# Attention's result transposed by VectorE in 32x32 blocks, and w_in's rows loaded in an order that matches

## The chip, the cores and the metric

The kernel runs on one core of a Trainium2 chip. A core has a matrix engine (TensorE, PE in the profile, with PEld for its weight loads), VectorE (DVE), ScalarE (ACT), GpSimd (POOL) and SyncE (SP), and 16 DMA engines that all queues share. SP and POOL issue nearly all transfers here. The metric is the device time of one execution in microseconds; lower is better. Every time below is in microseconds unless marked ns.

## The reference

Block-sparse attention over 4 batches, 8 heads, 768 positions and 64 channels a head, in blocks of 32 positions, followed by a feed-forward network of 512 to 2048 to 512 channels with an exact GELU:

```python
scores = scale * np.matmul(q, k.transpose(0, 1, 3, 2))
mask = np.abs(blk_i - blk_j) <= window                 # window = 1
mask = mask | (blk_i == 0) | (blk_j == 0) | (blk_i == n_blocks - 1) | (blk_j == n_blocks - 1)
for qb in range(n_blocks):
    for kb in sampled_blocks[qb]:                      # three drawn blocks for each
        mask[qb * block:(qb + 1) * block, kb * block:(kb + 1) * block] = True
attn = softmax(np.where(mask, scores, -1e9))
x = np.matmul(attn, v).transpose(0, 2, 1, 3).reshape(B * S, H * D)
h = x @ w_in
return (0.5 * h * (1.0 + erf(h / sqrt(2)))) @ w_out
```

So the first and the last block see everything (dense), and each of the other 22 sees its neighbours, the first, the last and three sampled blocks (sparse). Inputs are float32; the kernel computes in bfloat16 and accumulates in float32.

## The kernel before, in words

**Units.** The work is cut into eight units: one batch by one half of the positions (384 tokens). For each unit there is attention, which leaves `xT` (channels by tokens), then the first FFN product with GELU (`ffn1_step`, eight steps of two output tiles, 64 matmuls), then the second FFN product. The order of instructions on each engine is the order of the program; there is no scheduler. The second product of a unit is cut into 24 pieces of two matmuls (`ffn2_pieces`), which the next unit's attention draws one by one (`pieces`) to keep PE at work while it waits for others. The first unit has no such work, and draws idle matmuls instead (`idle_pieces`, L503).

**Groups and rounds.** A unit's attention has eight groups: two for the dense block, then five of two sparse blocks and one of a single one. A group passes through stages: scores on PE (`sc`, L339), a maximum on DVE (`nm`, L353 and L374), exponentials on ACT (`pp`, L385 and L388), transposes of the probabilities on PE (`tp`, L400) and their copy out of PSUM on ACT (`ps`, L407), the product with the values on PE (`av`, L431), and a division on DVE (`den`, `rec`, `xh`, L440 to L444). `attention` runs rounds `it`: in each, scores of group it+2, exponentials of it+1, transposes of group it, and the product of group it−`lag`. `lag` is 1, and 3 in the first unit, where values come late.

**From attention to `xT`.** `xh` has 32 queries times four pairs of heads on the partitions, and blocks and channels in columns. `stage_x` (L457 to L464) turns it one round later: one or two PE transposes of 128x128 into PSUM (`tx`, L459, from the pool `psT` that `tp` uses too), and a DVE copy into `xT` (L462). There is one more round for it at the end of a unit, with two pieces in front of it. The channels in `xT` then stand in their natural order, and so do `w_in`'s rows.

**Weights.** `load_w_in` loads columns 0 to 511, 512 to 1023 and 1024 to 2047 of `w_in` in three POOL DMAs, each for all four 128-row groups `ki`. The first is issued at the very start, the second after POOL's key copies (L632), the third after all value gathers of the first unit (L642).

**Values.** The values of a batch are written to a scratch in DRAM (L285) and read back: windows of neighbouring blocks (L310) and 33 gathers a unit of sampled blocks at places read from registers (L293). For the first unit SP and POOL share them; the second unit's (`second_values`) are all SP's. A memset by DVE in `second_values` (L651) writes the first window's place, so that SP's first window of the second unit waits for DVE to get there. POOL and SP each use eight completion semaphores in turn: a transfer waits for the one eight issues earlier on its queue.

## Time and profile before

| what | value |
|---|---|
| runs shown | 308.93 median of 3 (308.15 to 309.18) |
| profiled execution | 309.21, of which the span is 307.3 |
| PE busy | 284.0 (92%) |
| ACT busy | 207.8 (68%) |
| DVE busy | 197.1 (64%) |
| POOL busy | 126.7 (41%) |
| `tx` transposes on PE (L459) | 96, 14.8, 222 ns each |
| `xT` copies on DVE (L462) | 56, 14.9, 266 ns each |
| first FFN product on PE (L471) | 512, 88.6, 330 ns each |
| second FFN product on PE (L485) | 286 recorded, 81.9, 381 ns each |

The table shows busy time: for each engine the sum of the stretches in which it had work. A matmul's length includes the pipeline, so lengths of neighbours overlap, and what one matmul costs is better read from one start to the next. Lines of a timeline give the start, the length, the engine, the line and the tile written and read; in brackets stands how long the engine was idle before it and whose end it waited for. The granted clock of PE is a share of full speed. The first 60 microseconds hold the loads of the first batch, the first unit's attention and its first FFN product; from about 82 on one unit follows the other, some 33 apart.

### The profile page before, as it was taken

What the parts mean: (1) busy time and instruction counts of PE and PEld (TensorE: products, weight loads), DVE (VectorE), ACT (ScalarE), POOL (GpSimd) and SP (SyncE); (2) the same over time, 40 slices, a digit from 0 to 9 for tenths busy, and PEclk for the clock granted to TensorE, in tenths of its full rate; (3) what the DMA queues carried; (4) which work ended last, traced back from release to release, by engine and by line L of the source; (5) the groups of instructions that cost most, each with busy time, mean ns of one, the idle gap of its engine ahead of it and who ended that gap; (6) DMA issues with size and microseconds to landing.
All of it is one profiled execution on the core that took longest, in us unless ns stands there. A gap on an engine that the chain in (4) does not pass through costs nothing.

```text
span 307.3 us, 11604 instructions
## 1 busy us (share of the span) xinstructions
PE 284.0 (92%) x4476; PEld 173.0 (56%) x4526; DVE 197.1 (64%) x550; ACT 207.8 (68%) x443; POOL 126.7 (41%) x250
## 2 busy tenths in 40 slices
PE   6895969998999999999999989998999999999995
PEld 5443535555565566656565547555655656455784
DVE  6699454587594788878745868387818873684010
ACT  1485424588667896689668975788568965897620
POOL 8355926231556843824998172089603000000000
PEclk9999697999999999999999999999999999999999
DMA  7998899999278799799799958995632330000012
GB/s 94 197 217 149 182 209 228 228 225 194 87 234 176 166 215 222 267 253 200 186 242 168 229 111 282 260 241 145 174 81 63 64 101 3 35 4 36 34 36 68
DMA packets 55064, 48.45 MB, mean 158 GB/s; under 512 B 20385, under 2 KB 49058, under 8 KB 55010
## 3 DMA queue, kind: packets, MB, share of 16 engines
q1 hardware_dynamic: 35170, 30.86, 38.6%
q0 software_dynamic: 19408, 16.47, 33.6%
q8 instruction: 35, 0.57, 0.8%
q10 hardware_dynamic: 432, 0.39, 0.4%
q14 instruction: 19, 0.16, 0.2%
HBM read 45.63 MB, written 12.82 MB: 190 GB/s over the span
## 4 chain that ended last, share of the span: by engine, by line
PE 67%; ACT 12%; DMA 7%; issue 7%; SPq 2%; POOL 1%; DVE 1%; POOLq 0%; DVEq 0%
PE hp L471 28%; PE op L485 19%; ACT pp L385 8%; PE tp L400 5%; PE av L431 5%; PE sc L339 4%; PE op L519 3%; DMA w_in_sb<-in_moe_w_in_dram 3%; ACT ps L407 3%; DMA qn<-in_q_dram 3%; PE pt L245 2%; SPq L293 2%; PE tx L459 2%; DMA vscr<-vn 1%; ACT os L490 1%
## 5 line engine op out<-in xcount | busy, mean ns | idle before, releaser
L471 PE MATMUL hp<-xT,w_in_sb 128*128 128x384 bf16 x512 | 88.6, 330 | 2.4 <-DMA w_in_sb<-in_moe_w_in_dram 2.1
L485 PE MATMUL op<-w_out_sb,g 128*128 128x512 bf16 x286 | 81.9, 381 | 5.1 <-issue 4.6
L471 PEld LDWEIGHTS <-w_in_sb 128*128 128x128 bf16 x512 | 58.1, 115 | 30.7 <-DMA w_in_sb<-in_moe_w_in_dram 2.8
L475 ACT ACTIVATE g<-hp 128x768 bf16<-128x768 f32 x56 | 45.4, 811 | 38.5 <-PE hp L471 38.5
L385 ACT ACTIVATE pp<-sc,nm 128x256 bf16<-128x256 f32 x176 | 70.2, 492 | 0.0
L374 DVE TENSOR_REDUCE nm<-sc 128x4 f32<-128x1024 f32 (+1 forms) x48 | 54.5, 1135 | 12.1 <-ACT ps L407 10.3
L293 POOL DMA_DIRECT2D vg<-vscr x76 | 38.7, 513 | 35.9 <-PE sc L339 14.0
L407 ACT COPY ps<-tp 128x256 int32<-128x256 int32 (+2 forms) x114 | 36.1, 355 | 20.2 <-PE tp L400 18.4
L279 POOL COPY kg<-kT 128x128 bf16 x120 | 33.3, 332 | 30.3 <-PE sc L339 12.6
L400 PEld LDWEIGHTS <-pp 128*128 128x128 bf16 x448 | 31.2, 105 | 22.0 <-ACT pp L385 5.2
L400 PE MATMUL tp<-identity,pp 128*128 128x128 bf16 x448 | 40.3, 222 | 2.0
L485 PEld LDWEIGHTS <-g 128*128 128x128 bf16 x336 | 24.7, 97 | 21.9 <-issue 6.7
L353 DVE TENSOR_REDUCE nm<-sc 128x1 f32<-128x768 f32 x16 | 14.7, 952 | 31.8 <-PE sc L339 31.8
L431 PEld LDWEIGHTS <-ps 128*32 128x32 bf16 x1792 | 19.1, 97 | 18.9 <-issue 8.5
L431 PE MATMUL av<-vg,ps 128*32 128x65 bf16 x1408 | 21.4, 197 | 3.6 <-DMA vg<-vscr 2.4
L444 DVE TENSOR_TENSOR xh<-av,rec 128x256 bf16<-128x256 f32 (+1 forms) x56 | 21.6, 386 | 1.9
L462 DVE COPY xT<-tx 128x256 bf16<-128x256 bf16 (+1 forms) x56 | 14.9, 266 | 11.5 <-PE tx L459 11.4
L339 PE MATMUL sc<-kg,qT 64*32 64x256 bf16 (+1 forms) x704 | 18.7, 270 | 0.5 <-issue 0.5
L490 ACT COPY os<-op 128x512 f32<-128x512 f32 x21 | 12.3, 587 | 8.5 <-PE op L485 8.2
L279 DVE COPY kg<-kT 128x128 bf16 x144 | 17.5, 200 | 0.0
L271 DVE COPY kg<-kT 128x1408 bf16<-128x1408 bf16 x21 | 17.2, 875 | 0.0
L459 PEld LDWEIGHTS <-xh 128*128 128x128 bf16 x96 | 9.0, 98 | 14.1 <-DVE xh L444 6.4
(77 smaller groups left out, 276.2 us busy)
## 6 DMA issues: line engine op xcount, KB each, us to landing
vg<-vscr SPq DMA_DIRECT2D x188, 33.0 KB, 4.4
vg<-vscr SPq DMA_DIRECT2D x20, 297.0 KB, 5.2
out_dram<-os SPq DMA_DIRECT2D x21, 256.0 KB, 2.4
vscr<-vn SPq DMA_DIRECT2D x4, 792.0 KB, 4.7
kn<-in_k_dram POOLq DMA_DIRECT2D x8, 384.0 KB, 9.7
qn<-in_q_dram POOLq DMA_DIRECT2D x8, 384.0 KB, 11.0
vx<-in_v_dram POOLq DMA_DIRECT2D x8, 384.0 KB, 8.8
vg<-vscr POOLq DMA_DIRECT2D x76, 33.0 KB, 4.1
```

What stands on the lines that cost most here:

```text
L279: copy(kg[:, (j - 1) % US, :, 96 + BL * r:128 + BL * r], kTs[b % 2][:, :, bass.ds(vals[j, r] * BL, BL)])
L293: queue.dma_start(out=dst, in_=vscr[b][bass.ds(val * BL, BL), :])
L339: nc.tensor.matmul(out_, lhsT=qTs[b % 2][rows, h // 2, j * BL:(j + 1) * BL], rhs=rhs[rows], start=True, stop=True)
L374: nc.vector.tensor_reduce(out=nm[:, 0:2 * n].rearrange("p (j g) -> p j g", g=2), in_=A4[:, 0:n], op=ALU.max, axis=AX.X, negate=True)
L385: nc.scalar.activation(pp[:, 256 * n:256 * n + 256], A[:, c:c + 256], AF.Exp, bias=nm[:, n:n + 1])
L400: nc.tensor.transpose(T[:, c - c0, :], pp[:, cols], identity)
L407: copy(ps[:, c0:c1, :].rearrange("p c k -> p (c k)").bitcast(I32), T[:, 0:c1 - c0, :].rearrange("p c k -> p (c k)").bitcast(I32))
L431: nc.tensor.matmul(av[32 * hh:32 * hh + 32, s, :], lhsT=probs[:, 32 * hh:32 * hh + 32], rhs=vals[:, VW * h:VW * h + D + 1], start=(c == 0) ...
L444: nc.vector.tensor_tensor(xh[:, 0:n, :], av[:, 0:n, 0:D], rec[:, 0:n, None].to_broadcast([P, n, D]), op=ALU.mult)
L471: nc.tensor.matmul(hp[:, i, 0:UT], lhsT=w_in_sb[:, ki, c0:c0 + 512 - m % 4 - i:4], rhs=xT[:, ki, :], start=(ki == 0), stop=(ki == KIN - 1))
L475: nc.scalar.activation(g[:, m:m + 2, :], hp[:, :, 0:UT], AF.Gelu)
L485: nc.tensor.matmul(op, lhsT=g[:, m, t * P:(t + 1) * P], rhs=w_out_sb[:, m, :], start=(m == 0), stop=(m == KOUT - 1))
```

## The change

1. `stage_x` is gone. Right after the division, `stage_av` has DVE transpose `xh` in 32x32 blocks from SBUF into `xT`. This leaves each 32-channel block on the partitions of its pair of heads, so that row 32g + c of `xT`'s group k is channel 128g + 32k + c.
2. `load_w_in` takes one row group k and a range of columns, and reads `w_in`'s rows in that order: 128g + 32k + c. It is called for columns 0 to 511 four times at the start, and for columns 512 to 2047 four times among the value gathers of the first unit (after blocks 5, 7, 9 and 11). The loads of 512 columns after the key copies and of 1024 columns after the gathers are gone.
3. The first unit's `lag` is 4, and `ptpool` has six buffers.
4. `second_values` is called after the key copies of the second unit (`k_window`, `k_unit`); its memset moves with it on DVE.
5. The last round of `attention` is gone with `stage_x`; what is left of the pieces is drawn after the last product. The second unit draws one piece, not four, after its first exponential, none in round 2 and one more in round 6, and so keeps six for the end.

```diff
-    ptpool = ctx.enter_context(tc.tile_pool(name="ptpool", bufs=5))
+    ptpool = ctx.enter_context(tc.tile_pool(name="ptpool", bufs=6))
...
-    def load_w_in(part, n=1):
-        cols = slice(512 * part, 512 * (part + n))
-        nc.gpsimd.dma_start(out=w_in_sb[:, :, cols],
-                            in_=moe_w_in[:, cols].rearrange("(ko p) f -> p ko f", p=P))
+    def load_w_in(k, c0, c1):
+
+        nc.gpsimd.dma_start(
+            out=w_in_sb[:, k, c0:c1],
+            in_=bass.AP(tensor=moe_w_in.tensor, offset=moe_w_in.offset + BL * k * D_FF + c0,
+                        ap=[[P * D_FF, 4], [D_FF, BL], [1, c1 - c0]]))
...
-    load_w_in(0)
+    for i in range(KIN):
+        load_w_in(i, 0, 512)
...
-        st[grp] = xh
-
-    def stage_x(hf, grp):
-        xh = st.pop(grp)
...
-        T = psT.tile([P, 2, P], BF16, name="tx", tag="T")
-        for i in range(n):
-            nc.tensor.transpose(T[:, i, :], xh[:, 2 * i:2 * i + 2, :].rearrange("p g d -> p (g d)"),
-                                identity)
-        t0 = (js[0] - UB * hf) * BL
-        nc.vector.tensor_copy(
-            xT[:, :, t0:t0 + n * BL].rearrange("p h (j q) -> p j h q", j=n),
-            T[:, 0:n, :].rearrange("p j (h q) -> p j h q", h=4))
+
+        t0 = (grp[1] - UB * hf) * BL
+        nc.vector.transpose(xT[:, :, t0:t0 + n // 2 * BL].rearrange("p k (j q) -> p j k q", q=BL),
+                            xh[:, 0:n, :])
...
-        for it in range(-1, n + lag + 1):
+
+        second = (b, hf) == (0, 1)
+        for it in range(-1, n + lag):
...
-                pieces(3 if first else 4)
+                pieces(3 if first else 1 if second else 4)
...
-                elif not first and it == n + lag:
-                    pieces(2)
-                    stage_xs()
-                    pieces(KOUT)
...
-                if 2 <= it < n and it != n - 2 or (first and it < 2):
+                if 2 + second <= it < n and (it != n - 2 or second) or (first and it < 2):
...
-    load_w_in(1)
...
-        load_w_in(2, 2)
+                if j % 2 and j >= 5:
+                    load_w_in((j - 5) // 2, 512, D_FF)
...
             if u == 0:
-                second_values()
                 k_dve |= block_numbers(ids, J1[4:], RS, DVE)
...
                 k_unit(1, b, J1)
+                if u == 0:
+                    second_values()
...
-        attention(b, hf, filler, extra, later if u >= 0 else (), 1 if u >= 0 else 3)
+        attention(b, hf, filler, extra, later if u >= 0 else (), 1 if u >= 0 else 4)
```

More of the change, by code (lines that the diff above doesn't have):

```diff
@@ L445, in stage_av @@
                                 rec[:, 0:n, None].to_broadcast([P, n, D]), op=ALU.mult)
-        st[grp] = xh
-    def stage_x(hf, grp):
-        xh = st.pop(grp)
-        if grp[0] == "dense":
-            if grp[2] == 0:
-                return
-            js = (grp[1],)
-        else:
-            js = grp[1:]
-        n = len(js)
-        T = psT.tile([P, 2, P], BF16, name="tx", tag="T")
-        for i in range(n):
-            nc.tensor.transpose(T[:, i, :], xh[:, 2 * i:2 * i + 2, :].rearrange("p g d -> p (g d)"),
-                                identity)
-        t0 = (js[0] - UB * hf) * BL
-        nc.vector.tensor_copy(
-            xT[:, :, t0:t0 + n * BL].rearrange("p h (j q) -> p j h q", j=n),
-            T[:, 0:n, :].rearrange("p j (h q) -> p j h q", h=4))
+        t0 = (grp[1] - UB * hf) * BL
+        nc.vector.transpose(xT[:, :, t0:t0 + n // 2 * BL].rearrange("p k (j q) -> p j k q", q=BL),
+                            xh[:, 0:n, :])
     def ffn1_step(m):
@@ L545, in attention @@
                 stage_exp(groups[0])
-                pieces(3 if first else 4)
+                pieces(3 if first else 1 if second else 4)
             else:
-                def stage_xs():
-                    if 0 <= it - lag - 1 < n:
-                        stage_x(hf, groups[it - lag - 1])
-                if it < n + lag and not (first and it >= n):
-                    stage_xs()
                 if it == n or (first and it > n):
@@ L559, in attention @@
                     pieces(1)
-                elif not first and it == n + lag:
-                    pieces(2)
-                    stage_xs()
-                    pieces(KOUT)
-                elif first:
-                    stage_xs()
-                if it < n:
                     stage_transpose(groups[it])
```

## The prediction

> **What bounds the kernel now.** I read the split by engine first, then the table by stage, then the timeline of one undisturbed unit, and last the timelines of the start. The profiled execution took 309.21 us, a span of 307.3 and 1.91 around it; that is 0.28 above the median of the runs, 308.93. I sum against 309.21 and take 0.28 off at the end.

> ```profile
> PE 284.0 (92%) x4476; PEld 173.0 (56%) x4526; DVE 197.1 (64%) x550; ACT 207.8 (68%) x443; POOL 126.7 (41%) x250
> ...
> 17.00:35.60 18.60, 15.08 (x359) 8.10 (x357) 14.69 (x39) 11.95 (x33) 11.38 (x24) 0.83 0.90 195
> 45.20:59.30 14.10, 14.03 (x113) 8.51 (x115) 7.50 (x29) 5.91 (x8) 4.98 (x12) 0.88 1.11 225
> 261.00:282.80 21.80, 20.82 (x438) 11.53 (x442) 15.45 (x38) 18.92 (x47) 0.00 (x0) 1.00 0.07 27
> 282.80:293.20 10.40, 10.40 (x66) 7.32 (x65) 0.00 (x0) 6.26 (x8) 0.00 (x0) 1.00 0.07 25
> ```

> The columns of the stage rows are the stage, its length, busy time of PE, PEld, DVE, ACT and POOL, the granted clock, the DMA share and GB/s. The last two rows are a late unit: attention (21.8) and first FFN product (10.4). PE looks full in both. Two rows of the start have a lower clock, and DMA near or over 1 there.

> In a late attention the rounds go like this (start, length, what):

> ```profile
> 271.16 0.65 ACT L407 COPY ps<-tp 128x256 int32<-128x256 int32 x2 [0.21 <-PE tp L400]
> 271.70 1.59 ACT L385 ACTIVATE pp<-sc,nm 128x256 bf16<-128x256 f32 x4
> 273.50 0.65 ACT L407 COPY ps<-tp 128x256 int32<-128x256 int32 x2 [0.21 <-PE tp L400]
> ...
> 272.07 0.28 PE L459 MATMUL tx<-identity,xh 128*128 128x128 bf16 x2
> 272.27 0.43 PE L431 MATMUL av<-vg,ps 128*32 128x65 bf16 x32
> ...
> 271.83 1.22 DVE L374 TENSOR_REDUCE nm<-sc 128x4 f32<-128x1024 f32 x1 [0.18 <-ACT ps L407]
> 272.97 0.28 DVE L462 COPY xT<-tx 128x256 bf16<-128x256 bf16 x1
> ```

> ACT is almost never free: exponentials, then the copy of the transposed probabilities, then exponentials. In this round it waits 0.21 for PE. So PE and ACT are nearly level, and PE work taken out pays only while PE is the later one. The two `tx` transposes hold PE for 0.20 (272.07 to 272.27, the next start).

> The start:

> ```profile
> 30.11 0.65 PE L431 MATMUL av<-vg,ps 128*32 128x65 bf16 x20 [2.21 <-DMA vg<-vscr]
> 27.86 0.50 POOL L293 DMA_DIRECT2D vg<-vscr  x1 [1.69 <-DMA w_in_sb<-in_moe_w_in_dram]
> 35.62 0.81 POOL L152 DMA_DIRECT2D w_in_sb<-in_moe_w_in_dram  x1
> 42.84 0.32 PE L471 MATMUL hp<-xT,w_in_sb 128*128 128x384 bf16 x1 [0.32 <-DVE vg L651]
> 45.22 8.21 PE L471 MATMUL hp<-xT,w_in_sb 128*128 128x384 bf16 x39 [2.05 <-DMA w_in_sb<-in_moe_w_in_dram]
> 43.37 16.02 SPq L293 DMA_DIRECT2D vg<-vscr  x12
> ```

> PE waits 2.21 for the first gathered values, the gather queue on POOL waits 1.69 for a weight load, and the first FFN product does one matmul and then waits until the last weight load lands at 45.2, though it reads only columns 0 to 511. Last row: the second unit's gathers crawl.

> **The change, part by part.**

> *POOL at the very start.* The first load of `w_in` becomes four, and each issue takes the place of a DMA eight issues back: the third waits for the second half of K (10.3), the fourth for Q (11.97). Then 0.8 for the issue and three register loads (0.76, 0.94, 1.75 by the sequencer's rows) bring the key copies from 13.14 to 15.4. Scores want the first six copies at 17.27; six by 0.28 are done at 17.1. The 18 end at 20.4, and gathers can't start before 22.09 anyway (values land in scratch at 21.0). Cost nothing; if the cover is gone, 2.3.

> *First unit.* The second `w_in` load (issued 18.11) leaves the stretch in which the first window of values (issued 21.0, landed about 29.7) and the gathers compete. Values are used a round later, so PE should reach the first gathered product at about 29 without a wait. But the last product can't run before the last gather lands: 22.09, 19 gathers by 0.58 (11 took 6.39) and three weight issues by 0.79 among them give 35.5, and 4.3 from issue to landing (median) gives 39.8. The waits of 1.7 and 0.9 that the queue had may come back: 39.8 to 42.4. I take 40.5, since the load behind the longer wait is moved. From that product's start to the end of its transpose: 0.3 for the product, then 0.15 + 0.17 + 0.29 + 0.3 and gaps of 0.03 to 0.13: 1.4. FFN starts at 41.9, not 45.22.

> *FFN of unit 1.* 45.22 to 59.27 is 14.05. The first 39 matmuls took 8.21; at 0.163 (64 in 10.4) they would take 6.36, so 1.85 went to the half clock (0.50 granted in the stretch 46.5 to 47.0, after a near idle 42.5 to 45.2). After the change PE is some 40% busy from 33 to 41 (0.36 of products, 0.53 of idle matmuls in about 2.2). No row has that load, so 0 to 1.85 is saved and I take 0.95. [...] The first 16 matmuls need columns 0 to 511 alone. Matmul 17 onwards needs the last weight block, issued by 36.3 to 38.9: with the gathers' 4.3 it lands at 40.6, with the 9.6 of the three weight loads at 48.5. Needed at 44.5. That middle costs nothing; the late end costs 4. FFN ends at 55.0 instead of 59.27.

> *Second unit.* The memset that lets SP go on now stands behind the key copies, 6.5 later (42.73 against 49.3 where they end): 48.4. Queued behind it on SP are 3 windows and 33 gathers, then the output stores. From 59.45 to 75.43 SP issued 26 in 16.0, 0.615 each. Up to the values of the next to last group it is 33 by 0.615, 68.7, and 4.3 to land, 73.0. Before, the first window held the queue for 7.4 while weights and K were loading; most of those land earlier against it now, so 0 to 7.4, and I take 2: 75.0. PE wants them at 55.0 + 18.8 = 73.8 (78.08 − 59.27). So 1.2 of new wait. Behind that product three pieces of the second FFN product now stand at the end instead of the beginning: 6 matmuls by 0.216 = 1.3, which formerly hid a reduce and an exponential. From there to the next FFN: 3.8 + 1.3 − 0.2 of `tx` = 4.9. It starts at 79.9, not 81.9: **−2.0** so far, −3.2 to +3.4.

> *Units 3 to 8, PE.* Per unit go 0.15 + 4 × 0.20 + 0.11 + 0.07 = 1.13 of PE (12 `tx` in four kinds of place, each by the next start). ACT's own loop is 2.23 (exponentials at 267.15 and 269.38, no wait for PE); the rounds with `tx` took 2.32 and 2.33, and 2.59 with an output copy that ACT bounds. So 0.19 in rounds and 0.18 in the tail, where PE leads: 0.37. Ends: 0 and 1.13. Six units: **−2.2** (0 to −6.8).

> *Units 3 to 8, DVE.* The copy from PSUM (285 ns, 220 for the narrow one) goes; a 32x32 transpose SBUF to SBUF comes, behind the multiply it reads and ahead of the next reduce. No row has one. [...] I take 0.42 and 0.3. A DVE round is then 1.14 + 0.18 + 0.20 + 0.45 + 0.44 = 2.4 against 2.23 to 2.59, and a reduce that would start 0.25 late still ends 0.6 ahead of its exponential. [...] Behind the last product of a unit the four DVE steps take 1.25, covered by six matmuls of 1.30; from there on each 0.1 more of the narrow transpose costs 0.1 a unit, so at twice the multiply's 0.29 the tail's 0.18 is gone and 0.1 more: that end is 0.1 a unit left instead of 0.37.

> Sixth PSUM-copy buffer: no time. Sum: −2.0 − 2.2 = −4.2; 309.21 − 4.2 − 0.28 = **304.7**.

> **Rivals.**
> - *PE alone sets the rounds.* For it: PE 20.82 of 21.8. Against: no ACT idle but 0.2 a round. All 1.13 in six units, 4.6 more: 300.1.
> - *The last weight block is late.* Small loads behind gathers, each holding one of eight places. Lands at 48.5, 4 late, and the clock falls: FFN ends at 59.9, the unit at 59.9 + 18.8 + 4.9 = 83.6, +1.7 − 2.2: 308.4. For it: 9.5 to 11.6 of every weight load. Against: it is 384 KB in place, where those were 512, 512 and 1024. [...]
> - *Slower: the second unit's values are late.* SP starts 5.6 later and keeps its old pace (all of the 7.4): values at 80.4, next FFN at 85.3, +3.4 − 2.2: **310.1**. Level with before is reached when the queue loses 6.2 of the 7.4. For it: DMA share over 1.2 from 58 to 74. Against: the loads that blocked it are issued at 36 to 39 as before, and have 5.6 more to land before the gathers begin.

> **How the numbers follow.** Forecast 0.62, PE alone 0.14, weights late 0.10, values late 0.14. This kernel's runs can tell about 0.3%, 0.9 us. The forecast's own terms (−3.2 to 0 and 0 to −4) give 301.5 to 307; with the other cases 300.3 to 308.7, values late left out and most of the rest in. Faster: 0.62 less 0.02, 0.14 and half of 0.10: 0.79; same 0.07; slower 0.14.

> **What would show it.** Right: FFN of unit 1 starts near 42 with no weight wait before its 17th matmul; a late attention is 21.4 instead of 21.8; the transposes take 0.3 to 0.45; PE's busy time falls by some 15 with more idle time before `tp`. Wrong: PE idle before `av` in the second unit over 2; a late attention under 21 or over 21.8; the DVE reduce ending last before an exponential.

## The result, and the profile after

The change made the kernel slower: 324.29 us median (323.49 to 326.63) against 308.54 for the kernel before, run beside it. The ratio is 1.0525, with a 95% interval of 1.046 to 1.059. The prediction was 304.7. The profiled execution of the changed kernel took 324.97, with a span of 323.0; against 309.21 and 307.3 before, that is 15.8 longer.

Where FFN1 of each unit starts shows when the time was lost. FFN1 is the first FFN product. For unit 1 the row has its first long run of matmuls, since the kernel before ran one matmul earlier, at 42.84; for the other units it has the start that the chain of waits lists, which is 0.1 to 0.2 behind the timeline's.

| FFN1 of unit | before | after | after later by | gained or lost since the row above |
|---|---|---|---|---|
| 1 | 45.22 | 58.49 | 13.27 | +13.27 |
| 2 | 81.97 | 98.12 | 16.15 | +2.88 |
| 3 | 118.27 | 135.05 | 16.78 | +0.63 |
| 4 | 150.90 | 169.06 | 18.16 | +1.38 |
| 5 | 184.29 | 202.17 | 17.88 | −0.28 |
| 6 | 217.54 | 234.66 | 17.12 | −0.76 |
| 7 | 250.15 | 266.80 | 16.65 | −0.47 |
| 8 | 282.76 | 298.94 | 16.18 | −0.47 |
| end of span | 307.3 | 323.0 | 15.7 | −0.48 |

So nearly everything is lost by the end of the second unit's attention. From there on the two kernels are level (−0.45 in all), although undisturbed units are 0.47 shorter.

POOL's queue in the changed kernel, from the timeline (start, length, engine and line, what is issued, and in brackets the wait and whose end it waited for):

```profile
27.34 0.69 POOL L152 DMA_DIRECT2D w_in_sb<-in_moe_w_in_dram  x1
...
30.79 0.70 POOL L152 DMA_DIRECT2D w_in_sb<-in_moe_w_in_dram  x1
31.47 1.01 POOL L296 DMA_DIRECT2D vg<-vscr  x2
40.47 1.08 POOL L296 DMA_DIRECT2D vg<-vscr  x2 [7.98 <-DMA w_in_sb<-in_moe_w_in_dram]
41.54 0.70 POOL L152 DMA_DIRECT2D w_in_sb<-in_moe_w_in_dram  x1
42.23 2.18 POOL L296 DMA_DIRECT2D vg<-vscr  x4
44.40 0.69 POOL L152 DMA_DIRECT2D w_in_sb<-in_moe_w_in_dram  x1
...
54.62 0.71 POOL L159 DMA_DIRECT2D w_out_sb<-in_moe_w_out_dram  x1 [8.09 <-DMA w_in_sb<-in_moe_w_in_dram]
```

The four late weight loads that the change puts among the gathers are slow to land. The first, issued at 27.34, holds a gather up for 7.98. The last two are issued at 41.54 and 44.40, where the prediction had the last of them by 36.3 to 38.9. PE's timeline of the same kernel shows who pays:

```profile
40.60 0.36 PE L434 MATMUL av<-vg,ps 128*32 128x65 bf16 x12 [5.63 <-DMA vg<-vscr]
...
55.68 0.36 PE L434 MATMUL av<-vg,ps 128*32 128x65 bf16 x12 [11.44 <-DMA vg<-vscr]
...
58.49 1.79 PE L459 MATMUL hp<-xT,w_in_sb 128*128 128x384 bf16 x5 [1.14 <-DVE idx_DVE L221]
```

PE stands 5.63 and 11.44 for gathered values. The chain of waits of that stretch says the same of the gather itself:

```profile
42.73 12.91 DMA vg<-vscr
55.68 0.39 PE av L434 x9
```

A gather that takes 4.1 in the median of its queue took 12.9 here. And yet the DMA engines were not busy while POOL was held up. In the table by stage of the changed kernel (columns as in the prediction's stage rows; the last two are DMA share and GB/s):

```profile
36.00:38.00 2.00, 0.00 (x0) 0.00 (x0) 0.00 (x0) 0.00 (x0) 0.00 (x0) 0.82 0.56 119
38.00:40.00 2.00, 0.00 (x0) 0.00 (x0) 0.00 (x0) 0.00 (x0) 0.00 (x0) 0.50 0.53 121
```

And of the DMA queues of the changed kernel from 36 to 40 (packets, MB, share of the 16 engines):

```profile
q0 software_dynamic: 179, 0.38, 46.3%
q1 hardware_dynamic: 104, 0.10, 8.1%
```

POOL's queue is the software one: in the whole execution that queue carried 16.48 MB, and POOL's DMA issues add up to 16.46. What was left in it were the first two late weight loads (384 KB each) with gathers between and behind them. They kept less than half of the 16 engines busy. That is the clue that the experiments start from: the engines had room, so other transfers in the way do not explain how slow the loads were.

The steady part came out as forecast. VectorE's transposes, from the groups by form (count | busy, mean ns), and a late attention from the table by stage:

```profile
L451 DVE STREAM_TRANSPOSE xT<-xh 128x256 bf16<-128x256 bf16 x40 | 17.8, 445 | 1.4
...
L451 DVE STREAM_TRANSPOSE xT<-xh 128x128 bf16<-128x128 bf16 x16 | 5.0, 312 | 0.5
```

```profile
277.60:298.90 21.30, 20.89 (x432) 10.63 (x430) 16.35 (x38) 18.82 (x46) 0.00 (x0) 1.00 0.08 27
```

The two transposes take 445 and 312 ns, and a late attention 21.3 instead of 21.8.

### The profile page after: what moved, and what is told of

The parts are those of the page before. It is cut to its first block, busy times and chain, and to the rows that moved or that the text cites. A ratio compares the mean times of both kernels' runs of the same rounds, so it can differ in the third digit from the quotient of the medians.

```text
span 323.0 us, 11521 instructions
## 1 busy us (share of the span) xinstructions
PE 285.1 (88%) x4430; PEld 165.7 (51%) x4430; DVE 206.4 (64%) x550; ACT 207.0 (64%) x443; POOL 128.9 (40%) x255
## 2 busy tenths in 40 slices
DMA packets 57705, 48.47 MB, mean 150 GB/s; under 512 B 23537, under 2 KB 51698, under 8 KB 57650
## 3 DMA queue, kind: packets, MB, share of 16 engines
q0 software_dynamic: 22048, 16.48, 34.0%
## 4 chain that ended last, share of the span: by engine, by line
PE 53%; DMA 14%; DVE 14%; issue 9%; ACT 5%; SPq 2%; POOL 2%; DVEq 1%; POOLq 0%
PE hp L459 23%; PE op L473 16%; DMA vg<-vscr 10%; DVE nm L377 7%; PE sc L342 3%; PE op L507 3%; PE av L434 3%; PE tp L403 3%; DVE xh L447 3%; DMA qn<-in_q_dram 2%; ACT pp L388 2%; SPq L296 2%; DMA vscr<-vn 2%; ACT ps L410 2%; PE pt L248 1%
## 5 line engine op out<-in xcount | busy, mean ns | idle before, releaser
L473 PE MATMUL op<-w_out_sb,g 128*128 128x512 bf16 x336 | 91.7, 382 | 0.5 <-ACT os L478 0.5
L459 PE MATMUL hp<-xT,w_in_sb 128*128 128x384 bf16 x512 | 88.1, 330 | 1.1 <-DVE idx_DVE L221 1.1
L463 ACT ACTIVATE g<-hp 128x768 bf16<-128x768 f32 x56 | 45.4, 810 | 56.1 <-PE hp L459 56.1
L459 PEld LDWEIGHTS <-w_in_sb 128*128 128x128 bf16 x512 | 58.0, 115 | 28.7 <-issue 1.4
L377 DVE TENSOR_REDUCE nm<-sc 128x4 f32<-128x1024 f32 (+1 forms) x48 | 53.7, 1120 | 5.0 <-ACT ps L410 3.3
L296 POOL DMA_DIRECT2D vg<-vscr x76 | 38.0, 504 | 41.8 <-PE op L473 16.8
L410 ACT COPY ps<-tp 128x256 int32<-128x256 int32 (+2 forms) x114 | 36.5, 357 | 16.7 <-PE tp L403 14.0
L434 PEld LDWEIGHTS <-ps 128*32 128x32 bf16 x1792 | 20.2, 97 | 50.7 <-DMA vg<-vscr 18.4
L282 POOL COPY kg<-kT 128x128 bf16 x120 | 32.8, 322 | 32.7 <-PE sc L342 13.4
L434 PE MATMUL av<-vg,ps 128*32 128x65 bf16 x1408 | 23.8, 198 | 24.1 <-DMA vg<-vscr 18.9
L403 PE MATMUL tp<-identity,pp 128*128 128x128 bf16 x448 | 41.4, 220 | 3.9 <-ACT pp L391 1.1
L443 DVE TENSOR_SCALAR den<-av 128x4 f32<-128x4 f32 (+1 forms) x56 | 8.6, 154 | 34.9 <-PE av L434 34.6
L451 DVE STREAM_TRANSPOSE xT<-xh 128x256 bf16<-128x256 bf16 (+1 forms) x56 | 22.8, 407 | 1.9
L478 ACT COPY os<-op 128x512 f32<-128x512 f32 x21 | 12.3, 588 | 11.7 <-PE op L473 11.7
L282 DVE COPY kg<-kT 128x128 bf16 x144 | 19.2, 211 | 0.0
L342 PE MATMUL sc<-kg,qT 64*32 64x256 bf16 (+1 forms) x704 | 18.8, 269 | 0.4 <-POOL kg L282 0.4
L274 DVE COPY kg<-kT 128x1408 bf16<-128x1408 bf16 x21 | 17.1, 870 | 0.0
## 6 DMA issues: line engine op xcount, KB each, us to landing
qn<-in_q_dram POOLq DMA_DIRECT2D x8, 384.0 KB, 11.6
```

Source lines behind the costliest of these rows:

```text
L282: copy(kg[:, (j - 1) % US, :, 96 + BL * r:128 + BL * r], kTs[b % 2][:, :, bass.ds(vals[j, r] * BL, BL)])
L296: queue.dma_start(out=dst, in_=vscr[b][bass.ds(val * BL, BL), :])
L342: nc.tensor.matmul(out_, lhsT=qTs[b % 2][rows, h // 2, j * BL:(j + 1) * BL], rhs=rhs[rows], start=True, stop=True)
L377: nc.vector.tensor_reduce(out=nm[:, 0:2 * n].rearrange("p (j g) -> p j g", g=2), in_=A4[:, 0:n], op=ALU.max, axis=AX.X, negate=True)
L403: nc.tensor.transpose(T[:, c - c0, :], pp[:, cols], identity)
L410: copy(ps[:, c0:c1, :].rearrange("p c k -> p (c k)").bitcast(I32), T[:, 0:c1 - c0, :].rearrange("p c k -> p (c k)").bitcast(I32))
```

## The experiments

The theory after the result was about the address pattern of the changed loads. Before, a load's source was walked as 128 rows, then four row groups, then columns: `[[2048,128],[262144,4],[1,512]]`. After, it is `[[262144,4],[2048,32],[1,1536]]`: the outermost count is 4. **Theory A**: a load with 4 outermost moves over 4 of the 16 engines, so that two in flight keep 8 at most busy; this makes the loads slow, and the loss follows from that. Nothing read so far showed such a spread. It was a conjecture, which the software queue's 46.3% fits: 46.3% of 16 engines is 7.4. One rival: eight loads in place of three hold POOL's eight places, however they are spread. Another: VectorE's transposes or the second unit's moves cost it.

### 1 and 2: the same loads, outermost count 16 and 8

```diff
-            in_=bass.AP(tensor=moe_w_in.tensor, offset=moe_w_in.offset + BL * k * D_FF + c0,
-                        ap=[[P * D_FF, 4], [D_FF, BL], [1, c1 - c0]]))
+            in_=bass.AP(tensor=moe_w_in.tensor, offset=moe_w_in.offset + 8 * k * D_FF + c0,
+                        ap=[[32 * D_FF, 16], [D_FF, 8], [1, c1 - c0]]))    # 1
+            in_=bass.AP(tensor=moe_w_in.tensor, offset=moe_w_in.offset + 16 * k * D_FF + c0,
+                        ap=[[64 * D_FF, 8], [D_FF, 16], [1, c1 - c0]]))    # 2
```

> The changed kernel, except that the address pattern of each w_in load has 16 groups of 8 rows outermost in place of 4 groups of 32; calls, places, bytes and the contiguous run of each row are the same. The rows no longer match the channels of xT, so the output is not the reference's; the time is what is wanted. Theory A (a load whose pattern has 4 groups outermost moves over 4 of the 16 DMA engines, so that each late load takes 11.7 to 12.8 us, holds POOL's place of eight for 8.0 and 8.1 us and stands in front of the gathers): with 16 groups a late load lands in 5 to 7 us, both waits of POOL fall under 2 us, PE's 18.9 us of waiting for gathered values falls under 3, and the time is 302 to 307. Theory B (eight loads in place of three, put among the gathers, are what costs, whatever their pattern): the waits stay and the time is 321 to 326. Theory C (rows scattered over DRAM are slow to read): the rows are scattered here as well, 321 to 326.

> As the run before, with 8 groups of 16 rows outermost (output again not the reference's, since rows and channels don't match). Theory A: 8 engines, a late load in 6 to 8 us, POOL's waits between those of 4 and 16 groups, PE waiting 3 to 8 us for gathered values, time 306 to 314. Theories B and C: 321 to 326.

| outermost count | 4 (the change) | 8 | 16 |
|---|---|---|---|
| time | 324.29 | 316.18 | 312.02 |
| ratio to before | 1.0525 [1.046, 1.059] | 1.0215 [1.0154, 1.0276] | 1.0072 [1.0039, 1.0104] |
| median landing of the late loads | 12.7 | 7.8 | 6.1 |
| POOL's waits for w_in, 24 to 62 | 16.1 | 5.8 | 2.9 |
| PE's waits for gathered values in all | 18.9 | 9.2 | 4.5 |
| FFN1 of unit 2 | 98.12 | 87.38 | 82.92 |

The landing times come from the DMA issues of the changed kernel, of experiment 2 and of experiment 1, in that order (count, KB each, median us from issue to landing):

```profile
w_in_sb<-in_moe_w_in_dram POOLq DMA_DIRECT2D x4, 384.0 KB, 12.7
```

```profile
w_in_sb<-in_moe_w_in_dram POOLq DMA_DIRECT2D x4, 384.0 KB, 7.8
```

```profile
w_in_sb<-in_moe_w_in_dram POOLq DMA_DIRECT2D x4, 384.0 KB, 6.1
```

The same bytes in the same number of loads at the same places: the time falls with the count, and 12.3 of the 15.8 us are gone at 16. Eight loads as such are worth no more than what is left. Theory A's own times were missed all the same: 302 to 307 was expected at 16 and 306 to 314 at 8, and PE's waits for values were to be under 3 and from 3 to 8. Something else costs time too.

One thing goes along with the count: there are 1,024 more packets under 512 B at 8 than at 16, and 3,072 more at 4 (23,537 against 20,465), which carry 0.01 MB together. The single packets in the three traces tell the two apart. The rows of the four late loads are 512 packets of 3,072 bytes in each kernel, with the same median of 248 ns; most often about 4 or about 8 of them were under way at once at count 4 (one load or two in flight), about 8 at count 8 and about 16 at count 16. So each packet was as fast, and fewer went side by side, as theory A has it. The additional packets are of 4 bytes. All packets of that size on POOL's queue took 56.2 us of engine time in the changed kernel and 26.6 in experiment 1, 3.7 more for each of the eight loads. On four engines that is an estimated 0.9, and a late load landed 6.6 later.

### 3: w_in in quarters of 32 partitions

The row order that the change needs can also be had in loads whose outermost count is 32: each load takes 32 partitions for all four row groups. The columns lie in two tiles.

```diff
-            out=w_in_sb[:, k, c0:c1],
-            in_=bass.AP(tensor=moe_w_in.tensor, offset=moe_w_in.offset + BL * k * D_FF + c0,
-                        ap=[[P * D_FF, 4], [D_FF, BL], [1, c1 - c0]]))
+            out=(w_in_a if c0 == 0 else w_in_b)[BL * k:BL * k + BL],
+            in_=bass.AP(tensor=moe_w_in.tensor, offset=moe_w_in.offset + P * k * D_FF + c0,
+                        ap=[[D_FF, BL], [BL * D_FF, KIN], [1, c1 - c0]]))
```

> The changed kernel with the right rows on the right channels, but each load takes one quarter of the partitions (32) for all four row groups, so that 32 stands outermost on both sides; w_in is two tiles (columns 0 to 511, and the rest), so that the first 16 matmuls wait for the first tile alone. Same eight calls at the same places. Theory A: 302 to 307, late loads land in 5 to 7 us. Theories B and C: 320 to 326.

312.54 (310.97 to 314.44), ratio 1.0114 [1.0067, 1.016]. Theory A's 302 to 307 is missed here too. But with quite another pattern, and the row order that the change needs, the time is that of experiment 1 within 0.5, and a late load lands in 6.3 in the median: what counts in these runs is the outermost count. FFN1 of unit 1 starts at 42.48. The 3.9 us that are still missing against before (308.69 in these runs) lie behind it. PE's waits of this kernel from 56 to 84, the second unit's attention (in all, times, longest):

```profile
PE av L435 <- DMA vg<-vscr: 2.6, 2, 1.4
PE tp L404 <- ACT pp L392: 1.1, 1, 1.1
PE op L475 <- ACT os L480: 0.5, 1, 0.5
```

### 4: VectorE's transposes alone

The kernel before, with `nc.vector.transpose` in place of `stage_x`. The last round goes with `stage_x` (part 5); none of the other parts is in.

```diff
-        st[grp] = xh
-    def stage_x(hf, grp):
...
+        nc.vector.transpose(xT[:, :, t0:t0 + n // 2 * BL].rearrange("p k (j q) -> p j k q", q=BL),
+                            xh[:, 0:n, :])
```

> The kernel before with the transposes by VectorE alone: its three w_in loads in natural row order at their old places, values three rounds behind, pieces and second unit's values as before. Rows don't match the channels, so the output is not the reference's. If the transposes cost nothing and save what late units show (0.47 us each of six or seven, late unit 32.14 instead of 32.61), 305 to 307; if they cost in the first two units, over 309. All theories on the loads expect the first FFN product's long run to begin at 45 to 46 as before.

308.80 (307.64 to 312.97), ratio 0.999 [0.9966, 1.0015]: no change, so the expected 305 to 307 was missed. Two things stand in the way. FFN1 of unit 1 reaches its weights earlier and waits for them longer: 4.21 instead of 2.05, so that it starts at 44.62 instead of 45.22. And unit 4 took 35.8 (118.33 to 154.13) where the kernel before took 32.6. PE's timeline of this kernel, and its table by stage at the same place:

```profile
137.14 0.41 PE L339 MATMUL sc<-kg,qT 64*32 64x256 bf16 x16
...
138.96 1.01 PE L470 MATMUL op<-w_out_sb,g 128*128 128x512 bf16 x2 [1.41 <-issue]
```

```profile
138.00:139.00 1.00, 0.04 (x1) 0.04 (x1) 0.92 (x1) 1.00 (x3) 0.00 (x0) 0.89 0.95 215
139.00:140.00 1.00, 1.00 (x10) 0.17 (x13) 0.00 (x0) 0.09 (x1) 0.00 (x0) 0.50 1.24 150
140.00:141.00 1.00, 1.00 (x34) 0.63 (x35) 0.34 (x3) 0.00 (x0) 0.00 (x0) 0.50 0.99 221
141.00:142.00 1.00, 1.00 (x9) 0.72 (x8) 0.87 (x2) 0.04 (x1) 0.64 (x2) 0.50 1.28 291
```

PE stops for 1.41 in straight code and waits for nobody ("issue"). Then its granted clock is 0.50 for 3 us; by that clock about half of those is lost too, an estimate. The DMA queues of this kernel from 136.46 to 136.96 hold one packet of an instruction queue, amid a transposing DMA (`qT<-qscr`, 8.8 from issue to landing):

```profile
q1 hardware_dynamic: 258, 0.24, 138.3%
q8 instruction: 1, 0.02, 12.0%
```

That queue carried 35 packets and 0.57 MB in the whole execution, 16 KB each, for some 8,900 instructions of PE: one in 255. It is taken for PE's, since the engine with the next most, DVE, has 774 (in the changed kernel). **Theory D**: a block of PE's code came late behind other transfers, and where the blocks begin is chance.

### 5 and 6: the same, with PE's code moved on

```diff
-    for i in range(36):
+    for i in range(28):          # 6: 20
         nc.tensor.transpose(idle[:, i % 6, :], identity, identity)
+    for i in range(40):          # 6: 80
+        nc.tensor.transpose(idle[0:32, i % 6, 0:32], identity[0:32, 0:32], identity[0:32, 0:32])
```

> Transposes alone (the fourth run's kernel) with 32 small transposes more in PE's idle work at the start, so that PE's program is 64 instructions longer ahead of everything else and nothing else differs. As in the fourth run, w_in's rows stay in their old order, so the FFN's values are not the reference's. In the fourth run unit 4 took 35.8 us (118.33 to 154.13) where its neighbours took 32.7 to 33: PE stood for 1.41 us at 137.5 with 'issue' as the reason, in the middle of straight code, and then ran at a clock of 0.50 from 139 to 142. Theory D: PE's code comes in blocks of 16 KB (35 packets on the instruction queue for some 8,900 instructions of PE, one in 255), one of them came late behind a burst of DMA work, and the stop let the clock fall; where the blocks' borders lie is chance. Then the stop leaves its place: unit 4 takes 32.5 to 33.2 and the time is 305.0 to 306.5, unless another block is late elsewhere. Rival: the stop belongs to unit 4's data (the transposing DMAs at 130 to 141) or to the missing PE transposes: unit 4 takes 35.5 to 36 again and the time is 308.3 to 309.3.

> The same with 64 small transposes more for full ones taken out (44 more in all, 88 instructions longer; w_in's rows in their old order here too). Theory D: the stop of 1.4 us with the half clock behind it is not at unit 4's place, or is at another; time 305.0 to 306.5 if no block is late, 308 to 309 with one late block elsewhere, and the trace shows a packet of the instruction queue just ahead of any such stop. Rival: unit 4 takes 35.5 to 36 as before, time 308.3 to 309.3.

The second of the two is in fact 128 instructions longer (64 transposes more, each with a weight load); the count in its expectation is wrong. Experiment 5: 310.31, ratio 1.0056 [1.0023, 1.0088]. Experiment 6: 308.76, 0.9976 [0.9938, 1.0015]. The first is above all that was expected; the second lies where theory D has it with one late block elsewhere, and where its rival has it too. The stop left its place: in experiment 5 unit 4 took 32.5 (119.43 to 151.95), and PE went through the spot with 0.16 of wait. But another block came late, in unit 6, on which the time hung instead. PE's timeline of experiment 5 at the old place and at the new one:

```profile
138.80 0.38 PE L470 MATMUL op<-w_out_sb,g 128*128 128x512 bf16 x1 [0.16 <-issue]
...
209.79 0.27 PE L339 MATMUL sc<-kg,qT 64*32 64x256 bf16 x1 [2.01 <-issue]
```

An instruction packet lies between 206.79 and 207.29 there, amid a busy queue, as theory D has it; the clock was then 0.50 to 0.52 from 210 to 213. In experiment 6 a stop of 1.47 came at 112 without loss of clock (1.00 from 112 to 113), and unit 4 was long again (36.3) for another reason, a wait of 2.33 for gathered values that ended at 147.4. So the stop belongs to the place in the code and not to unit 4's data; the expected 305 did not come because the stops moved and did not go.

### 7: the second unit as before the change

Experiment 3 with `second_values` back ahead of the registers, and the second unit's pieces where all other units have them.

```diff
-        second = (b, hf) == (0, 1)
+        second = False
...
             if u == 0:
+                second_values()
                 k_dve |= block_numbers(ids, J1[4:], RS, DVE)
...
-                if u == 0:
-                    second_values()
```

> The third run's kernel (the whole change with w_in in quarters of 32 partitions) with the second unit put back as it was before the change: its values fetched ahead of the registers and key copies, four pieces of FFN work ahead of its first round and none in its third last. The third run's PE waited 1.19 and 1.41 us for the second unit's values, 1.14 for its first exponentials and 0.45 for ACT. Theory: these 4.2 us are the two moves' price; unit 2's FFN starts at 79 to 80.5 (third run 83.15, before 81.97) and the time is 308.0 to 309.8. Rival: the values are late because of the transfers themselves, not of where they are issued: 311.5 to 313 as in the third run.

308.58 (306.61 to 310.72), ratio 1.0004 [0.9961, 1.0047], 4.0 under experiment 3 (3.4 by the two ratios). FFN1 of unit 2 starts at 80.70 instead of 83.15, just behind the expected 79 to 80.5. PE's waits of this kernel from 56 to 84:

```profile
PE av L435 <- DMA vg<-vscr: 2.9, 4, 1.9
PE op L475 <- issue: 0.8, 5, 0.2
PE av L435 <- issue: 0.2, 1, 0.2
```

The waits for the first exponentials (1.1) and for ACT (0.5) are gone. Those for values are not (2.9 against 2.6): the unit now comes to them earlier. So the second unit's moves are the rest of the loss. How much of it is the values' place, to which the expectation gave 2.6, the waits do not tell.

### 8: quarters at the old places

VectorE's transposes with the matching row order and none of the moves: each of the three old loads split in four.

```diff
-    load_w_in(1)
+    for i in range(KIN):
+        load_w_in(i, 512, 1024)
...
-        load_w_in(2, 2)
+        for i in range(KIN):
+            load_w_in(i, 1024, D_FF)
```

> The kernel before with VectorE's transposes and w_in in quarters of 32 partitions, each of the three loads split into four at its old place; values three rounds behind, five buffers, second unit as before: the transposes' part of the change with none of its moves, and a correct row order. Theory: the loads at their old places land as in the kernel before, FFN1 of the first unit still waits for the last block as in the fourth run (44.6), and the time is that run's, 308.0 to 309.3, or 305 to 306.5 if no block of PE's code comes late in it. Rival: twelve loads in place of three hold POOL's queue longer (9 more issues of 0.55 us, 5 us of which half lie ahead of gathers): FFN1 at 46 to 48 and 310 to 312.

309.57 (308.49 to 312.73), ratio 1.0039 [1.0, 1.0078]: just above the theory's numbers. FFN1 starts at 39.87, but in its 18th matmul it waits for weights; PE's timeline of this kernel:

```profile
42.49 0.33 PE L462 MATMUL hp<-xT,w_in_b 128*128 128x384 bf16 x1
45.40 5.55 PE L462 MATMUL hp<-xT,w_in_b 128*128 128x384 bf16 x23 [2.58 <-DMA w_in_b<-in_moe_w_in_dram]
```

Loads behind all the gathers land at 45.4, as in the kernel before (45.2), and PE waits for them. Experiment 7, with the loads among the gathers as the change has them, starts the same matmuls at 41.88 and 44.51 without a wait for weights. By the whole time the two places cannot be told apart: the intervals of the ratios, this one and 1.0004 [0.9961, 1.0047], overlap.

### 9: the second unit's fetches back, its pieces as changed

```diff
             if u == 0:
+                second_values()
                 k_dve |= block_numbers(ids, J1[4:], RS, DVE)
...
-                if u == 0:
-                    second_values()
```

> The third run's kernel (whole change, w_in in quarters) with only the second unit's fetches put back ahead of the registers and key copies; its pieces of FFN work stay as the change puts them (one ahead of the first round, one more in the third last). The seventh run, with both put back, took 308.6 where the third took 312.5. If the fetches' place is the price: 308.3 to 309.8, and the waits of 1.19 and 1.41 us for values in the second unit go down by the 1.8 us that the fetches start earlier. If the pieces' place is: 311.5 to 313, with the 1.14 us wait for the first exponentials still there. If both share it: 310 to 311.3.

311.26 (308.46 to 314.29), ratio 1.0072 [1.0027, 1.0117], between experiments 3 (1.0114) and 7 (1.0004): what was expected if both share the price. By the medians the fetches' place costs 1.3 and the pieces' place 2.7, but the interval takes in experiment 3's ratio and comes near to 7's, so the split is not settled; only the sum is. The waits in its trace fit a shared price too. From 56 to 85 PE waits 0.9 for values, where experiment 3 had 2.6: a fall of 1.7, about the 1.8 expected of the fetches' place. The 1.1 for the first exponentials and the 0.5 for ACT stayed. But the trace is of an execution of 313.75, 2.5 above the median, whose first FFN1 began only at 46.05, and it does not settle the split either.

### 10 and 11: experiment 7 with PE's code moved on

The edits of 5 and 6, on experiment 7.

> The seventh run's kernel (quarters, first unit four rounds behind, second unit as before the change) with 32 small transposes more in PE's idle work at the start: only the places where PE's code blocks begin move. In the seventh run PE stood for 1.22 us at 113.2 and ran at half clock from 115 to 119; unit 3 took 38.8 (80.70 to 119.51) where the kernel before took 36.3. Theory: the stop moves, and with it some 2.5 to 3.3 us: 305 to 306 if no stop of over 1.2 us comes elsewhere, 308 to 309.5 if one does. Rival (the stop belongs to unit 3's transfers, wherever the blocks begin): unit 3 takes 38.5 to 39 again, 308.3 to 309.

> The same with 80 small transposes for 16 full ones (64 transposes, 128 instructions more). The same theories and numbers: 305 to 306 if no stop of over 1.2 us comes, 308 to 309.5 with one, at another place than in the seventh run; the rival 308.3 to 309 with unit 3 at 38.5 to 39.

Experiment 10: 310.57 (308.19 to 311.88), ratio 1.0029 [0.9986, 1.0072], above all that was expected. Its stops over 1.2 were at 114.3 (1.21) and 211.1 (2.25), each with the clock at 0.50 behind it. Unit 3 took 38.4, as long as the rival had it; but in experiments 11 and 12, with the same transfers, it took 36.5 and 35.8, so the rival fails. Experiment 11: 307.45 (306.01 to 311.34), ratio 0.9946 [0.9898, 0.9995], between the two times expected. PE's timeline of experiment 11 holds these stops for "issue" in units 3 to 8, and no others over 0.5:

```profile
112.71 0.42 PE L435 MATMUL av<-vg,ps 128*32 128x65 bf16 x31 [0.80 <-issue]
...
178.97 0.24 PE L435 MATMUL av<-vg,ps 128*32 128x65 bf16 x7 [1.43 <-issue]
```

Neither cost clock. Its profiled execution took 306.61, near its fastest. Experiment 11 is ahead of both kernels, of the one before by half a per cent. The interval hardly excludes 1, and of the three placements of the code that were tried this is the best, so part of it is luck. Experiment 11 holds the change's transposes, its lag and its early places for the loads; it has not its address pattern nor its second unit. The count of idle transposes at the start, with no work done by them, decided some 3 us between 10 and 11.

### 12: more idle work in the first unit

Experiment 11 waits for values in the first unit and its clock falls there.

```diff
                 if it == n or (first and it > n):
-                    pieces(1)
+                    pieces(2 if first else 1)
```

> The eleventh run's kernel (quarters, first unit four rounds behind, second unit as before the change, PE's code moved on by 128 instructions; 307.45 us) with one more pair of idle matmuls ahead of the values' products in each of the first unit's last four rounds, and eight small transposes fewer at the start, so that the code behind the first unit stands where it stood. In the eleventh run PE waited 0.89, 0.56, 0.41 and 1.88 us for values there and its clock was 0.50 from 39 to 48, into FFN1. If the idle work holds the clock up: FFN1 of the first unit runs its first 40 matmuls in 6.8 to 7.5 us instead of 8.43, unit 2's FFN starts at 80.2 to 81.2 and the time is 306.0 to 307.2. If the waits are too long for it, or the idle work itself delays the products: 307.3 to 308.5. Against the kernel before: faster by 0.5 to 1 per cent, or the same.

308.05 (305.41 to 310.94), ratio 0.9965 [0.9933, 0.9997]: no gain on experiment 11, as expected if the waits are too long for the idle work. FFN1's first 40 matmuls took 8.04, not 6.8 to 7.5. PE's timeline of this kernel:

```profile
41.98 0.28 PE L435 MATMUL av<-vg,ps 128*32 128x65 bf16 x12 [2.14 <-DMA vg<-vscr]
...
44.61 4.14 PE L461 MATMUL hp<-xT,w_in_a 128*128 128x384 bf16 x16 [1.15 <-DVE vg L632]
```

The idle work was done before the wait of 2.14 and not in it. The clock was still 0.50 to 0.51 from 44 to 47, and unit 2's FFN1 started at 81.66. One more pair of idle matmuls ahead of each product did not cover it.

## Why the prediction was wrong

- **The failed step is "First unit".** It let the queue's old waits of 1.7 and 0.9 come back and had the last gather land between 39.8 and 42.4. The queue's waits were 7.98 ahead of a gather and 8.09 behind the last, and the values landed at 55.6. The prediction priced a changed load by the rows of loads with another address pattern; the pattern's outermost count, 4, stood in the diff. The step put FFN1 at 41.9 and it began at 58.49: 16.6 of the 19.6 by which the forecast was short. That the last gather sets FFN1's start was right, and the price of the loads in front of it was wrong. With that count at 32 and the second unit put back, FFN1 starts at 41.88 (experiment 7). That this meets the step to 0.02 is luck: with the same loads it started at 42.48 to 46.05 in experiments 3 and 9 to 12.
- **FFN of unit 1, 0.95 saved for the clock.** Both ends of its 0 to 1.85 came. In experiment 7 the granted clock was 1.00 from 33 to 48, and all of it was saved. In experiments 3, 11 and 12 it was 0.50 in FFN1 (42 to 44, 44 to 48 and 45 to 47 us), though PE's longest waits ahead of it were 1.4, 1.9 and 2.1 there and 1.6 in experiment 7. What decides between the two no run here shows.
- **The last weight block.** "40.6 to 48.5", with the late end as a rival at 308.4. The load was issued only at 44.40. The rival named the right place, but its size came from the same rows: it let the load be late for FFN1, and not hold the gathers that share its queue.
- **Second unit, 1.2 of new wait and 1.3 for the pieces.** Together 2.5; experiments 3 and 7 give 4.0 for the two moves. In the changed kernel itself PE's waits from 60 to 98 are 1.6 for values, 1.1 for the first exponentials and 0.5 for ACT; in experiment 3 they are 2.6, 1.1 and 0.5. So the pieces' part came near its price, the values' part was up to twice the term, and the 0.5 for ACT was in no term. The rival "values late" (5.4 above the forecast) had the right sign and place. Its wait is not cured by undoing the moves (2.9 in experiment 7), since the unit comes to its values earlier then.
- **Units 3 to 8, −0.37 each.** Undisturbed late units gained 0.47 (32.61 to 32.14), and the transposes' 0.42 and 0.3 were 0.445 and 0.312: right. The two numbers taken for the transposes stood in no row before; close to them lay the multiply's 0.424 and 0.291. The sum of −2.2 did not come: −0.45. Units 3 and 4 lost 2.0; PE stops for late code there, for 2.4 in all. The stops over 0.5 in units 3 to 8 sum to 3.2 in the changed kernel and 1.1 in the kernel before. No step of the prediction had them.
- **PE's busy time** was to fall by some 15; it went from 284.0 to 285.1. The two profiles do not count alike: 286 of the 336 matmuls of the second FFN product are recorded before (81.9) and all 336 after (91.7). Besides, a matmul at half clock counts as longer (FFN1's took up to 527 ns in unit 1 before, at 0.50 from 47 to 49, and 326 in the last unit at 1.00), and lengths of neighbours overlap (those 326 ns against one start every 163). As a test this was useless.
- **Two slips in the sums**, of no weight. The terms for the key copies add up to 16.2, not 15.4; the copies began at 15.94, and PE waited 0.40 for them at 17.85. And the forecast's ends, −3.2 to 0 and 0 to −4, give 301.7 to 308.9 from 308.93, not 301.5 to 307.

The balance by medians: 12.3 for the loads' pattern (the changed kernel against experiment 1; 14 by the two ratios), 4.0 for the second unit's moves (3 against 7; 3.4 by the ratios), and nothing that can be told for all the rest together (7 against before: 1.0004). The gain in late units and the earlier start of the first FFN are there in experiment 7's trace; its unit 3, with a stop of 1.22 and the half clock behind it, takes 2.5 back (38.8 against 36.3). Why the kernel before has only short stops in units 3 to 8 (0.53 and 0.54) is not settled; experiments 5, 6, 10 and 11 show that the places matter, not what a good place is.

## What to carry to other kernels

Read a changed load's address pattern as the queue sees it: a reordering that puts a count of 4 outermost cost 12 us here, and the same order with 32 outermost did not. A slow transfer on a queue of eight places was paid for by what stood behind it (7.98 and 8.09 of wait here), so price a moved load together with the gathers that it is moved among. Before a gain of 1% is credited to an edit of an unrolled kernel, shift the code by some idle instructions: here that alone moved the time by some 3 us (experiments 10 and 11).
